# Query projections of a fused attention and expert kernel: two whole-array heads per product, or half-array products of 64 rows

## The chip, the cores and the metric

The kernel runs on one core of a Trainium2 chip. The time is the device time of one execution in microseconds (us), the median of several runs. The core's engines are TensorE (PE in the profile, its weight loads apart as PEld), VectorE (DVE), ScalarE (ACT), GpSimd (POOL) and SyncE (SP, which issues most transfers).

## The reference

Three layers follow each other: attention with a feature map, a gated feed-forward layer, and a layer of slot experts. The change is in the first.

```python
def phi(x):                                   # x: q or k, (4, 8, 576, 64)
    proj = einsum('bhsd,df->bhsf', x, w_phi)  # 64 -> 128 features
    proj = proj - max(abs(proj), axis=-1)
    return concatenate([exp(proj), exp(-proj)], axis=-1)
q_p, k_p = phi(q), phi(k)
kv  = einsum('bhsf,bhsd->bhfd', k_p, v);  z = sum(k_p, axis=2)
num = einsum('bhsf,bhfd->bhsd', q_p, kv)
den = einsum('bhsf,bhf->bhs', q_p, z) + 1e-6
x = num / den                                 # -> 2304 tokens x 512
xn = x / sqrt(mean(x*x) + 1e-6) * rms_g       # gated layer
x = (silu(xn @ w_gate) * (xn @ w_val)) @ w_out
...                                           # slot experts on x
```

## The kernel before, in words

The 2304 tokens are cut into 18 tiles of 128 and into 6 blocks of 384 (three tiles each). The program has three stages.

The **key loop** (lines 502 to 697, to about 123 us of the trace) runs over the 18 tiles. For each it loads the keys and values, projects the keys (`Front.project`, line 519; VectorE then takes the largest value per row, `mx`, and subtracts it into `pr`), takes the exponentials `kp` on ScalarE, and adds to `kacc` (lines 571 and 580). Two things are laid into this loop. One is the conversion of the weights of the gated layer into two float32r parts (class `Conv`: `wt` on ScalarE and VectorE, the casts of line 119 on ScalarE, the low parts of line 122 on GpSimd). The other is the whole attention of query block 0, class `Rows`.

The **gated layer** (lines 738 to 1062) runs over the six blocks. Each block has twelve rounds of a `pg` group (12 products of 384 columns), a `pv` group (12 more) and an `acc` group (9 products of 512 columns). After each group `fill` calls what is planned for that slot, 36 slots per block. Into its first block (123 to 221 us) the attention of query block 1 is laid, class `Turned`; the later query blocks are projected in another way (`Reduced`, `Added`) and are not touched. The **slot experts** come last.

Query blocks 0 and 1 have their features on the columns and their tokens on the partitions. A query tile of heads is `qraw`: two heads' 64 rows one above the other, 384 tokens. There are four of them per block, one per column group c. `project` (line 409) makes one product per token tile i: 128 rows against `wbd_f`, a block diagonal matrix of 128 x 256, so both heads' 128 features come out side by side, and half of what is multiplied is zero. VectorE takes the largest of each head's row (`qmx`, line 415) and subtracts it (`qpr`, line 416). `turn` (line 421) transposes the two heads on TensorE (`T`, line 427) and ScalarE takes the exponentials into `e` (line 429). `attend` makes numerator and denominator: in `Rows` with tokens on the partitions (`o`, line 472, then `y`), in `Turned` with tokens on the columns (`num`, `den`, lines 221 and 249). `scale` and `out` normalize and, in `Rows`, transpose `y` back into `xraw`, the input of the gated layer.

A float32 product is recorded as two instructions (passes) on TensorE, so 24 projections are 48 records. The keys' projection (line 526) is already written with half the array: heads of 64 rows, those of even heads in the upper half and those of odd heads in the lower.

When a step may run is set by two tables, `TURNED0` for block 0 (in half-steps of the key loop) and `TURNED1` for block 1 (in slots). A scheduler then orders each engine's instructions. `P`, `T`, `o`, `yT`, `num` and `den` share an accumulator tag, "misc", with three buffers.

Of the kernel before, what the change touches and what calls it, by code (L numbers as in the profile page):

```python
# [7 lines left out]
F32 = mybir.dt.float32  # L8
F32R = mybir.dt.float32r
U32 = mybir.dt.uint32  # L10
AF = mybir.ActivationFunctionType
ALU = mybir.AluOpType
AX = mybir.AxisListType
# [3 lines left out]
NB, NH, SEQ, HD, DF = 4, 8, 576, 64, 128  # L17
NT, DM, DFF = 2304, 512, 1536
# [3 lines left out]
BLK = 384  # L22
NBLK = NT // BLK
TPB = BLK // 128
# [12 lines left out]
ADDED = [-3, -3, -1, 0, 2, 3, 6, 1, 5, 4, 8, 9, 12, 6, 11, 9, 14, 15, 18, 12, 17, 15, 20, 21, 25, 26, 28, 31]  # L37
TURNED0 = [2, 8, 14, 20, 12, 15, 20, 26, 28, 31]
TURNED1 = [0, 7, 14, 21, 6, 13, 20, 26, 28, 30]

# [25 lines left out]
def tile_kernel(ctx: ExitStack, tc: tile.TileContext, q2T, qT, kT, v, wbd, wg, wv, wo, rmsg, phi, w1, w2, consts, out):  # L66
# [32 lines left out]
    xp = pool(qctx, "xp", side="right")  # L99
# [91 lines left out]
    xraw = {}  # L191
# [209 lines left out]
    class Turned(Q):  # L401
# [6 lines left out]

        def project(self, c, i):
            p = self.psum("P", [128, 2, DF])  # L410
            o = p.rearrange("p h f -> p (h f)")
            PE.matmul(out=o, lhsT=self.raw[c][:, 128 * i:128 * i + 128], rhs=wbd_f, start=True, stop=True)
            mx = self.sp.tile([128, 2, 1], F32, tag="mx", name="qmx", bufs=2)
            self.pr = self.sp.tile([128, 2, DF], F32, tag="pr", name="qpr", bufs=self.bufs["pr"])
            DVE.tensor_reduce(out=mx, in_=p, axis=AX.X, op=ALU.max, apply_absolute_value=True)
            DVE.tensor_tensor(out=self.pr, in0=p, in1=mx.to_broadcast([128, 2, DF]), op=ALU.subtract)
            if i == TPB - 1:
                self.load(c + self.bufs["raw"])
            return self.pr

        def turn(self, c, i, pr):
            if i == 0:
                self.e2 = self.sp.tile([128, 2, 2, BLK], F32, tag="e", name="e2", bufs=self.bufs["e"])
                self.e[2 * c], self.e[2 * c + 1] = self.e2[:, 0], self.e2[:, 1]
            tp = self.psum("T", [128, 2, 128])
            for h in range(2):
                PE.transpose(out=tp[:, h], in_=pr[:, h], identity=ident)
            for s in range(2):
                ACT.activation(out=self.e2[:, :, s, 128 * i:128 * i + 128], in_=tp, func=AF.Exp, scale=1.0 - 2.0 * s)
# [13 lines left out]

        def steps(self, at, attend, end, lag=2):


            r, pr = [], {}

            def p(c, i):
                pr[c, i] = self.project(c, i)  # L450

            for c in range(4):
                for i in range(TPB):
                    r.append((at[c] + i, lambda c=c, i=i: p(c, i)))
                    r.append((at[c] + i + lag, lambda c=c, i=i: self.turn(c, i, pr[c, i])))
                r.append((attend[c], lambda c=c: self.attend(c)))
            r += [(end[0], self.scale), (end[1], self.out)]
            return sorted(r, key=lambda x: x[0])

    class Rows(Turned):  # L460


        def attend(self, c):
            if c == 0:
                self.y = self.sp.tile([128, TPB, 4, 2, HD], F32, tag="y", name="y", bufs=1)
            e = [self.e.pop(2 * c), self.e.pop(2 * c + 1)]
# [9 lines left out]
            DVE.reciprocal(out=rd, in_=rd)  # L476
            DVE.tensor_tensor(out=self.y[:, :, c], in0=o[:, :, :, 0:HD], in1=rd.to_broadcast([128, TPB, 2, HD]), op=ALU.mult)
            for b, t0, t1 in block_parts(self.blk):
# [4 lines left out]
        def scale(self):  # L483
            sq = self.sp.tile([128, 2, 2, BLK], F32, tag="e", name="sq", bufs=self.bufs["e"]).rearrange("p a b t -> p (a b t)")
            ms = self.sp.tile([128, TPB], F32, tag="ms", name="ms", bufs=1)
            rows = [self.y[:, i].rearrange("p c h d -> p (c h d)") for i in range(TPB)]
            for i in range(TPB):
                ACT.activation(out=sq[:, DM * i:DM * i + DM], in_=rows[i], func=AF.Square, accum_out=ms[:, i:i + 1])
            DVE.tensor_scalar(out=ms, in0=ms, scalar1=1.0 / DM, scalar2=1e-6, op0=ALU.mult, op1=ALU.add)
# [4 lines left out]
        def out(self):  # L494
            xraw[self.blk] = xp.tile([128, 4, BLK], F32, tag="xraw", name="xraw", bufs=1)
            for c in range(4):
                tp = self.psum("yT", [128, TPB, 128])
                for i in range(TPB):
                    PE.transpose(out=tp[:, i], in_=self.y[:, i, c].rearrange("p h d -> p (h d)"), identity=ident)
                ACT.activation(out=xraw[self.blk][:, c].rearrange("p (i t) -> p i t", i=TPB), in_=tp, func=AF.Copy, scale=rms_sb[:, c:c + 1])  # L500

    with ExitStack() as pk:
# [146 lines left out]
        q0 = Rows(sp, psk, 0, {"misc": 3, "raw": 2, "pr": 3, "e": 2})  # L649
        qsteps = q0.steps(TURNED0[0:4], TURNED0[4:8], TURNED0[8:])  # L650
        qsteps = [[f for m, f in qsteps if m == n] for n in range(2 * TILES)]
# [86 lines left out]
    with ExitStack() as p2:  # L738
# [233 lines left out]
        steps = []  # L972
        q = Turned(q1p, ps, 1, {"misc": 3, "raw": 2, "pr": 4, "e": 1})
        q.begin()
        qnext = q.steps(TURNED1[0:4], TURNED1[4:8], TURNED1[8:], lag=3)
        for _ in range(2):
# [235 lines left out]
```

## Time and profile before

| | |
|---|---|
| runs | 728.85, 731.23, 732.27 us; median 731.23 |
| the profiled execution | 730.81 us, its span 729.0 us, mean granted TensorE clock 0.991 of full speed |
| TensorE | busy 706.5 us (97%), 4713 products |
| VectorE | busy 447.2 us (61%) |
| ScalarE | busy 340.5 us (47%) |
| projections `P` of query blocks 0 and 1 (line 412) | 48 records, 379 ns each |
| keys' projections `P` (line 526) | 288 records, 272 ns each |
| transposes `T` (line 427) | 48 records, 272 ns each |

The duration of one product includes its way through the array, which overlaps the next product. What a product costs in a stream is read from when the next one starts, or from the chain's pieces. The span is the time from the first to the last instruction of the profiled execution.

### The profile page before, as it was taken

The numbers are of one execution on the slowest core, as the hardware profiler recorded it, in microseconds if no ns is written. First come the engines' busy times: TensorE is split into PE (matmuls) and PEld (weight loads), VectorE is DVE, ScalarE is ACT, GpSimd is POOL, SyncE is SP. The second block draws the span as 40 slices with busy tenths as digits, with TensorE's granted clock in tenths as the row PEclk, the third lists the DMA queues.
The fourth block names the chain that finished last, engine by engine and source line by source line (L and its number), as shares of the span: only waits on it lengthen the run. The fifth ranks groups of instructions, "written<-read, shape, count | busy, mean of one in ns | idle before, by whom it ended". The sixth has DMA issues, their size and how long they took to land.

```text
span 729.0 us, 11925 instructions
## 1 busy us (share of the span) xinstructions
PE 706.5 (97%) x4713; PEld 575.7 (79%) x4713; DVE 447.2 (61%) x874; ACT 340.5 (47%) x711; POOL 170.2 (23%) x84
## 2 busy tenths in 40 slices
PE   6999999999999999999999999999999999999994
PEld 4657766988889888898889888899887999898343
DVE  5899755798655565566776666766667653233313
ACT  5896755698444554355531545415454131212103
POOL 0233200234101210124443244342443300000000
PEclk9999999999999999999999999999999999999898
DMA  8684214443011000100000100001000066576798
GB/s 315 215 293 171 88 37 160 150 181 119 1 62 39 27 22 23 39 22 22 23 1 9 44 22 23 1 9 33 23 1 1 9 259 260 201 261 265 280 371 273
DMA packets 25143, 79.43 MB, mean 109 GB/s; under 512 B 2688, under 2 KB 13376, under 8 KB 18688
## 3 DMA queue, kind: packets, MB, share of 16 engines
q1 hardware_dynamic: 24864, 77.79, 30.0%
q10 hardware_dynamic: 224, 0.88, 0.4%
q8 instruction: 37, 0.61, 0.3%
q14 instruction: 18, 0.15, 0.1%
HBM read 71.99 MB, written 6.67 MB: 108 GB/s over the span
## 4 chain that ended last, share of the span: by engine, by line
PE 84%; DVE 7%; ACT 4%; issue 2%; POOL 1%; DMA 1%; SPq 0%; DVEq 0%; POOLq 0%; ACTq 0%
PE pv L938 20%; PE pg L938 19%; PE acc L963 6%; PE acc L964 6%; PE acc L965 6%; PE num L221 4%; PE kacc L571 4%; PE y L1084 2%; PE P L526 2%; PE kacc L580 2%; PE y L1100 2%; DVE wt L154 2%; DVE wt L156 1%; PE o L472 1%; ACT wt L144 1%
## 5 line engine op out<-in xcount | busy, mean ns | idle before, releaser
L938 PE MATMUL pv<-xnh,wv 128*128 128x384 f32 x576 | 152.3, 345 | 0.0
L938 PE MATMUL pg<-xnh,wg 128*128 128x384 f32 x576 | 150.1, 342 | 0.5 <-DVE t L946 0.3
L938 PEld LDWEIGHTS pv<-xnh,wv 128*128 128x128 f32 x576 | 102.7, 188 | 12.3 <-issue 7.8
L938 PEld LDWEIGHTS pg<-xnh,wg 128*128 128x128 f32 x576 | 104.7, 188 | 6.2 <-ACT xnh L119 0.6
L938 PE MATMUL pv<-xnl,wv 128*128 128x384 f32 x288 | 97.8, 340 | 0.0
L938 PE MATMUL pg<-xnl,wg 128*128 128x384 f32 x288 | 97.5, 339 | 0.0
L963 PE MATMUL acc<-wo,hh 128*128 128x512 f32 x216 | 88.9, 412 | 0.0
L306 POOL PARTITION_ALL_REDUCE qe<-qe x32 | 51.3, 1603 | 155.1 <-ACT qe L305 155.1
L964 PE MATMUL acc<-wo,hh 128*128 128x512 f32 x216 | 85.8, 397 | 0.0
L965 PE MATMUL acc<-wo,hl 128*128 128x512 f32 x216 | 85.5, 396 | 0.0
L946 DVE SCALAR_TENSOR_TENSOR t<-t,pg 128x384 f32<-128x384 f32 x72 | 39.7, 551 | 70.1 <-ACT t L945 70.0
L119 ACT CAST hh<-t 128x384 fp32r<-128x384 f32 x72 | 36.8, 511 | 94.3 <-PE acc L964 73.6
L351 POOL PARTITION_ALL_REDUCE qe<-qe x24 | 61.9, 2626 | 71.3 <-DVE qe L350 41.8
L122 DVE TENSOR_TENSOR hl<-t,hh 128x384 fp32r<-128x384 f32 x72 | 41.8, 581 | 54.7 <-ACT hh L119 45.5
L945 ACT ACTIVATE t<-pg 128x384 f32<-128x384 f32 x72 | 35.2, 489 | 63.8 <-PE pg L938 63.7
L950 DVE TENSOR_TENSOR t<-t,pv 128x384 f32<-128x384 f32 x72 | 39.5, 549 | 30.3 <-PE pv L938 29.7
L938 PEld LDWEIGHTS pg<-xnl,wg 128*128 128x128 f32 x288 | 54.0, 188 | 0.5 <-DVE xnl L122 0.3
L938 PEld LDWEIGHTS pv<-xnl,wv 128*128 128x128 f32 x288 | 54.0, 188 | 0.4 <-issue 0.3
L965 PEld LDWEIGHTS acc<-wo,hl 128*128 128x128 f32 x216 | 40.5, 188 | 9.9 <-DVE hl L122 0.3
L963 PEld LDWEIGHTS acc<-wo,hh 128*128 128x128 f32 x216 | 40.7, 189 | 7.9 <-ACT hh L119 0.9
L964 PEld LDWEIGHTS acc<-wo,hh 128*128 128x128 f32 x216 | 40.7, 189 | 6.4
L571 PE MATMUL kacc<-kp,vt 128*64 128x256 f32 (+1 forms) x320 | 43.2, 393 | 1.9 <-ACT kp L548 1.4
(213 smaller groups left out, 1099.7 us busy)
## 6 DMA issues: line engine op xcount, KB each, us to landing
eu<-in_w_dram SPq DMA_DIRECT2D x32, 1024.0 KB, 6.5
wraw<-in_wg_dram SPq DMA_DIRECT2D x6, 1024.0 KB, 5.0
wraw<-in_wv_dram SPq DMA_DIRECT2D x6, 1024.0 KB, 5.4
wraw<-in_wo_dram SPq DMA_DIRECT2D x6, 1024.0 KB, 4.9
qraw<-in_qT_dram SPq DMA_DIRECT2D x32, 192.0 KB, 2.4
raw<-in_kT_dram SPq DMA_DIRECT2D x18, 256.0 KB, 3.9
vt<-in_v_dram SPq DMA_DIRECT2D x18, 256.0 KB, 3.5
out_dram<-ob SPq DMA_DIRECT2D x18, 256.0 KB, 3.2
```

Of the source, the lines that this page charges most:

```text
L119: ACT.copy(out=hi, in_=src)
L122: (lo_eng or POOL).tensor_tensor(out=lo, in0=src, in1=hi.bitcast(F32), op=ALU.subtract)
L306: POOL.partition_all_reduce(e[:, 0], e[:, 1], channels=128, reduce_op=bass_isa.ReduceOp.absmax)
L351: POOL.partition_all_reduce(e[hh][:, 1], u, channels=128, reduce_op=bass_isa.ReduceOp.add)
L571: PE.matmul(out=kva[o0:o0 + 64, hh // 2], lhsT=self.vt[r0:r1, h], rhs=kp[r0:r1, hh].rearrange("p s f -> p (s f)"), start=first and hh < 2, ...
L938: PE.matmul(out=p, lhsT=w[:, a, c], rhs=x, start=n == 0, stop=n == 11)
L945: ACT.activation(out=t, in_=g, func=AF.Tanh, scale=0.5)
L946: DVE.scalar_tensor_tensor(out=t, in0=t, scalar=1.0, in1=g, op0=ALU.add, op1=ALU.mult)
L950: DVE.tensor_tensor(out=t, in0=t, in1=wide("v", m, xs), op=ALU.mult)
L963: PE.matmul(out=acc[i], lhsT=hh[:, s], rhs=w[:, 0], start=m == 0, stop=False)
L964: PE.matmul(out=acc[i], lhsT=hh[:, s], rhs=w[:, 1], start=False, stop=False)
L965: PE.matmul(out=acc[i], lhsT=hl[:, s], rhs=w[:, 0], start=False, stop=m == MF - 1)
```

## The change

It concerns query blocks 0 and 1 alone. A step now takes two column groups at once, index k, and makes four products of 64 rows for a token tile: the upper heads of the two groups go to one accumulator, the lower heads to another. The largest value and the subtraction are taken per accumulator, so their number and size stay. There are 6 steps per block with two accumulators each, where there were 12 with one. `pr` holds two groups (four heads). `turn` takes its group out of it. The tables now give a place for each of the six projections, for each group's turn, and for attend, scale and out. The projections of groups 0 and 1 come together at the front and those of groups 2 and 3 in the middle; the two later `qraw` loads go out together. In `Rows` the tile `y` is gone: attend writes to `xraw`, scale works in it, and out transposes it in place.

```diff
-TURNED0 = [2, 8, 14, 20, 12, 15, 20, 26, 28, 31]
-TURNED1 = [0, 7, 14, 21, 6, 13, 20, 26, 28, 30]
+TURNED0 = [[2, 3, 4], [14, 15, 16]], [4, 8, 16, 20], [12, 15, 20, 26], [28, 31]
+TURNED1 = [[0, 1, 2], [10, 12, 15]], [3, 8, 17, 22], [6, 13, 20, 26], [28, 30]
...
-        def project(self, c, i):
-            p = self.psum("P", [128, 2, DF])
-            o = p.rearrange("p h f -> p (h f)")
-            PE.matmul(out=o, lhsT=self.raw[c][:, 128 * i:128 * i + 128], rhs=wbd_f, start=True, stop=True)
-            mx = self.sp.tile([128, 2, 1], F32, tag="mx", name="qmx", bufs=2)
-            self.pr = self.sp.tile([128, 2, DF], F32, tag="pr", name="qpr", bufs=self.bufs["pr"])
-            DVE.tensor_reduce(out=mx, in_=p, axis=AX.X, op=ALU.max, apply_absolute_value=True)
-            DVE.tensor_tensor(out=self.pr, in0=p, in1=mx.to_broadcast([128, 2, DF]), op=ALU.subtract)
+        def project(self, k, i):
+            p = [self.psum("P", [128, 2, DF]) for _ in range(2)]
+            for c in range(2):
+                for hf in range(2):
+                    r = slice(64 * hf, 64 * hf + 64)
+                    PE.matmul(out=p[hf][:, c], lhsT=self.raw[2 * k + c][r, 128 * i:128 * i + 128], rhs=wbd_f[r, DF * hf:DF * hf + DF], start=True, stop=True)
+            pr = self.sp.tile([128, 2, 2, DF], F32, tag="pr", name="qpr", bufs=self.bufs["pr"])
+            for hf in range(2):
+                mx = self.sp.tile([128, 2, 1], F32, tag="mx", name="qmx", bufs=2)
+                DVE.tensor_reduce(out=mx, in_=p[hf], axis=AX.X, op=ALU.max, apply_absolute_value=True)
+                DVE.tensor_tensor(out=pr[:, :, hf], in0=p[hf], in1=mx.to_broadcast([128, 2, DF]), op=ALU.subtract)
             if i == TPB - 1:
-                self.load(c + self.bufs["raw"])
-            return self.pr
+                for c in range(2):
+                    self.load(2 * k + c + self.bufs["raw"])
+            return pr
...
-                PE.transpose(out=tp[:, h], in_=pr[:, h], identity=ident)
+                PE.transpose(out=tp[:, h], in_=pr[:, c % 2, h], identity=ident)
...
-        def steps(self, at, attend, end, lag=2):
+        def steps(self, at, turn, attend, end):
...
+            for k in range(2):
+                for i in range(TPB):
+                    r.append((at[k][i], lambda k=k, i=i: p(k, i)))
             for c in range(4):
                 for i in range(TPB):
-                    r.append((at[c] + i, lambda c=c, i=i: p(c, i)))
-                    r.append((at[c] + i + lag, lambda c=c, i=i: self.turn(c, i, pr[c, i])))
+                    r.append((turn[c] + i, lambda c=c, i=i: self.turn(c, i, pr[c // 2, i])))
...
-                self.y = self.sp.tile([128, TPB, 4, 2, HD], F32, tag="y", name="y", bufs=1)
+                xraw[self.blk] = xp.tile([128, 4, BLK], F32, tag="xraw", name="xraw", bufs=1)
...
-            DVE.tensor_tensor(out=self.y[:, :, c], in0=o[:, :, :, 0:HD], in1=rd.to_broadcast([128, TPB, 2, HD]), op=ALU.mult)
+            DVE.tensor_tensor(out=xraw[self.blk][:, c].rearrange("p (i h d) -> p i h d", i=TPB, h=2), in0=o[:, :, :, 0:HD], in1=rd.to_broadcast([128, TPB, 2, HD]), op=ALU.mult)
...
-                    PE.transpose(out=tp[:, i], in_=self.y[:, i, c].rearrange("p h d -> p (h d)"), identity=ident)
+                    PE.transpose(out=tp[:, i], in_=xraw[self.blk][:, c, 128 * i:128 * i + 128], identity=ident)
...
-        q = Turned(q1p, ps, 1, {"misc": 3, "raw": 2, "pr": 4, "e": 1})
+        q = Turned(q1p, ps, 1, {"misc": 3, "raw": 2, "pr": 3, "e": 1})
```

The order of the instructions follows. In its rows a line gives the program's line, the operation, what is written from what, the shape of the result and a count. Lines of the changed program are two to four higher than those of before.

TensorE in the key loop, from the third tile's kacc on, before (`P` from `qraw` is a query projection, `P` from `raw` a key projection):

```order
L580 MATMUL kacc_194<-kp,small 32x256 x7
L412 MATMUL P<-wbd_f,qraw 128x256 x2
L571 MATMUL kacc_192<-kp,vt 64x256 x3
L526 MATMUL P<-wbd_f,raw 128x128 x8
L571 MATMUL kacc_192<-kp,vt 64x256
L571 MATMUL kacc_193<-kp,vt 64x256 x4
L580 MATMUL kacc_194<-kp,small 32x256 x8
L427 MATMUL T<-cst,qpr 128x128 x2
L412 MATMUL P<-wbd_f,qraw 128x256
```

and with the change:

```order
L583 MATMUL kacc_194<-kp,small 32x256 x7
L414 MATMUL P<-wbd_f,qraw 128x128 x6
L574 MATMUL kacc_192<-kp,vt 64x256
L529 MATMUL P<-wbd_f,raw 128x128 x7
L414 MATMUL P<-wbd_f,qraw 128x128 x2
L529 MATMUL P<-wbd_f,raw 128x128
L574 MATMUL kacc_192<-kp,vt 64x256 x3
L574 MATMUL kacc_193<-kp,vt 64x256 x4
L583 MATMUL kacc_194<-kp,small 32x256 x8
L414 MATMUL P<-wbd_f,qraw 128x128 x4
L431 MATMUL T<-cst,qpr 128x128 x2
```

Three steps of four products take the place of three products. The first step and the first half of the second (one row group) stand together; the second half stands among the keys' products.

TensorE in the first round of the gated layer, around the first acc group, before:

```order
L938 MATMUL pv<-xnl_1429,wv_390 128x384
L412 MATMUL P<-wbd_f,qraw 128x256
L963 MATMUL acc_1474<-wo_545,hh 128x512
L964 MATMUL acc_1474<-wo_545,hh 128x512
L965 MATMUL acc_1474<-wo_545,hl 128x512
...
L965 MATMUL acc_1476<-wo_545,hl 128x512
L412 MATMUL P<-wbd_f,qraw 128x256
L938 MATMUL pg<-xnh_1416,wg_692 128x384 x2
```

and with the change:

```order
L941 MATMUL pv<-xnl_1434,wv_413 128x384
L414 MATMUL P<-wbd_f,qraw 128x128 x2
L966 MATMUL acc_1479<-wo_567,hh 128x512
L414 MATMUL P<-wbd_f,qraw 128x128 x2
L967 MATMUL acc_1479<-wo_567,hh 128x512
L968 MATMUL acc_1479<-wo_567,hl 128x512
...
L968 MATMUL acc_1481<-wo_567,hl 128x512
L414 MATMUL P<-wbd_f,qraw 128x128 x4
L941 MATMUL pg<-xnh_1421,wg_695 128x384 x2
```

Each former single product is a group of four half-array products between whole-array ones; here one such group is split in two.

ScalarE ahead of the third attend's numerator in the same block, before (`e` from `T` are the exponentials, `xraw` from `num` is the first reading of the numerator):

```order
L945 ACTIVATE t<-pg 128x384
L429 ACTIVATE e_1947<-T 128x2x128 x2
L119 CAST wo_2234<-wt 128x1024
L429 ACTIVATE e_1947<-T 128x2x128 x2
L119 CAST hh<-t 128x384
L251 COPY xraw<-num 128x384
```

and with the change:

```order
L948 ACTIVATE t<-pg 128x384
L433 ACTIVATE e_1976<-T 128x2x128 x2
L119 CAST wv_2155<-wt 128x1024
L433 ACTIVATE e_1976<-T 128x2x128 x2
L119 CAST wo_2245<-wt 128x1024
L119 CAST hh<-t 128x384
L251 COPY xraw<-num 128x384
```

The last exponentials have moved ahead of the cast of wo; the cast of wv has moved between the last two pairs.

## Rows read from the trace of the kernel before

**Rows 1.** The page, part 1: busy time, share of the span and instructions of each engine.
```profile
PE 706.5 (97%) x4713; PEld 575.7 (79%) x4713; DVE 447.2 (61%) x874; ACT 340.5 (47%) x711; POOL 170.2 (23%) x84
```

**Rows 2.** Stages: us, then busy us of PE, PEld, DVE, ACT, POOL; PEclk; DMA share, GB/s.
```profile
20.00:40.00 20.00, 20.00 (x192) 11.85 (x194) 18.39 (x26) 16.60 (x28) 5.85 (x3) 1.00 0.66 222
40.00:60.00 20.00, 18.72 (x188) 13.04 (x182) 19.56 (x29) 17.91 (x31) 6.52 (x3) 1.00 0.72 258
...
80.00:100.00 20.00, 20.00 (x216) 13.33 (x212) 12.85 (x27) 10.31 (x24) 4.69 (x2) 1.00 0.19 54
...
125.00:150.00 25.00, 25.00 (x156) 22.80 (x155) 19.27 (x26) 17.93 (x29) 7.22 (x3) 1.00 0.52 180
```

**Rows 3.** Timeline, PE, key loop: start, us, engine, line, xcount [idle before <- releaser].
```profile
44.50 0.70 PE L412 MATMUL P<-wbd_f,qraw 128*128 128x256 f32 x2 [1.28 <-DVE kv L617]
...
72.34 1.95 PE L571 MATMUL kacc<-kp,vt 128*64 128x256 f32 x16 [0.49 <-ACT kvs L595]
```

**Rows 4.** Timeline, PE and then ACT, gated layer: num of the third attend.
```profile
185.49 0.87 PE L221 MATMUL num<-e,kv 128*64 128x192 f32 x8 [1.20 <-ACT e L429]
...
185.06 0.65 ACT L429 ACTIVATE e<-T 128x256 f32<-128x256 f32 x2
```

**Rows 5.** Chain in order of time: start, us, engine, line, count of instructions.
```profile
128.21 2.12 PE pg L938 x12
132.45 0.43 PE P L412 x2
...
204.22 2.33 PE pg L938 x12
```

**Rows 6.** Timeline, PE, key loop: half-array groups and what follows each.
```profile
28.00 1.16 PE L526 MATMUL P<-wbd_f,raw 64*128 64x128 f32 x8
29.08 0.65 PE L571 MATMUL kacc<-kp,vt 128*64 128x256 f32 x2
...
36.86 1.16 PE L526 MATMUL P<-wbd_f,raw 64*128 64x128 f32 x16
37.95 1.94 PE L571 MATMUL kacc<-kp,vt 64*64 64x256 f32 x16
```

**Rows 7.** Timeline, PE, 40 to 46 us: a half-array group of four passes.
```profile
45.13 0.49 PE L526 MATMUL P<-wbd_f,raw 64*128 64x128 f32 x4
```

**Rows 8.** Chain, kvt groups; then the lines table, kv copies on VectorE.
```profile
80.62 0.59 PE kvt L608 x4
...
121.35 1.47 PE kvt L608 x12
...
L617 DVE COPY kv<-kvt 128x256 f32<-128x256 f32 x4 | 1.7, 422 | 0.7 <-ACT kv L619 0.7
```

**Rows 9.** Timeline, PE, start of the gated layer; then the chain, one acc product.
```profile
123.47 0.61 PE L938 MATMUL pg<-xnh,wg 128*128 128x384 f32 x2 [0.23 <-ACT xnh L119]
...
133.59 0.23 PE acc L963
```

**Rows 10.** Timeline, ACT, 172 to 188 us: the cast of wo.
```profile
184.11 1.04 ACT L119 CAST wo<-wt 128x1024 fp32r<-128x1024 f32 x1 [2.96 <-DVE wt L156]
```

**Rows 11.** Timeline, DVE, key loop.
```profile
19.89 1.29 DVE L530 TENSOR_REDUCE mx<-P 128x4 f32<-128x512 f32 x2 [0.92 <-PE P L526]
...
22.29 0.75 DVE L415 TENSOR_REDUCE qmx<-P 128x2 f32<-128x256 f32 x2
22.95 0.75 DVE L416 TENSOR_TENSOR qpr<-P,qmx 128x256 f32<-128x256 f32 x2
...
24.63 1.29 DVE L530 TENSOR_REDUCE mx<-P 128x4 f32<-128x512 f32 x2 [0.93 <-PE P L526]
...
29.19 0.69 DVE L530 TENSOR_REDUCE mx<-P 128x4 f32<-128x512 f32 x1 [0.61 <-PE P L526]
```

**Rows 12.** Timeline, PE and ACT, around the first attend of block 1.
```profile
145.92 0.86 PE L249 MATMUL den<-e,kv 128*32 128x192 f32 x16
...
154.02 0.53 ACT L228 ACTIVATE s<-xraw 128x384 f32<-128x384 f32 x1
```

More of the change, by code (lines that the diff above doesn't have):

```diff
@@ L442, in begin, with p @@
                 self.load(c)
-        def steps(self, at, attend, end, lag=2):
+        def steps(self, at, turn, attend, end):
             r, pr = [], {}
-            def p(c, i):
-                pr[c, i] = self.project(c, i)
+            def p(k, i):
+                pr[k, i] = self.project(k, i)
+            for k in range(2):
+                for i in range(TPB):
+                    r.append((at[k][i], lambda k=k, i=i: p(k, i)))
             for c in range(4):
                 for i in range(TPB):
-                    r.append((at[c] + i, lambda c=c, i=i: p(c, i)))
-                    r.append((at[c] + i + lag, lambda c=c, i=i: self.turn(c, i, pr[c, i])))
+                    r.append((turn[c] + i, lambda c=c, i=i: self.turn(c, i, pr[c // 2, i])))
                 r.append((attend[c], lambda c=c: self.attend(c)))
@@ L485, in scale @@
             ms = self.sp.tile([128, TPB], F32, tag="ms", name="ms", bufs=1)
-            rows = [self.y[:, i].rearrange("p c h d -> p (c h d)") for i in range(TPB)]
+            rows = [xraw[self.blk][:, :, 128 * i:128 * i + 128] for i in range(TPB)]
             for i in range(TPB):
-                ACT.activation(out=sq[:, DM * i:DM * i + DM], in_=rows[i], func=AF.Square, accum_out=ms[:, i:i + 1])
+                ACT.activation(out=sq[:, DM * i:DM * i + DM].rearrange("p (c t) -> p c t", c=4), in_=rows[i], func=AF.Square, accum_out=ms[:, i:i + 1])
             DVE.tensor_scalar(out=ms, in0=ms, scalar1=1.0 / DM, scalar2=1e-6, op0=ALU.mult, op1=ALU.add)
@@ L494, in out @@
         def out(self):
-            xraw[self.blk] = xp.tile([128, 4, BLK], F32, tag="xraw", name="xraw", bufs=1)
             for c in range(4):
@@ L649, in tile_kernel @@
         q0 = Rows(sp, psk, 0, {"misc": 3, "raw": 2, "pr": 3, "e": 2})
-        qsteps = q0.steps(TURNED0[0:4], TURNED0[4:8], TURNED0[8:])
+        qsteps = q0.steps(*TURNED0)
         qsteps = [[f for m, f in qsteps if m == n] for n in range(2 * TILES)]
@@ L972, in tile_kernel @@
         steps = []
-        q = Turned(q1p, ps, 1, {"misc": 3, "raw": 2, "pr": 4, "e": 1})
+        q = Turned(q1p, ps, 1, {"misc": 3, "raw": 2, "pr": 3, "e": 1})
         q.begin()
-        qnext = q.steps(TURNED1[0:4], TURNED1[4:8], TURNED1[8:], lag=3)
+        qnext = q.steps(*TURNED1)
         for _ in range(2):
```

## The prediction

> **What bounds the kernel now.** I read the page's busy shares first, then the table of stages, then where TensorE waits. TensorE is busy 97% of the span and VectorE 61% [rows 1]. TensorE's granted clock is 1.00, its upper level (2.4 GHz), in every stretch that I use [rows 2]. So a change counts if it shortens TensorE's own list or the few waits in it. The projections sit in two stages: block 0's in the key loop (to about 123 us), block 1's in the first block of the gated layer (123 to 221 us). The table shows that they differ. From 20 to 60 us VectorE is nearly as full as TensorE (18.39 and 19.56 of 20 us); from 80 us on it has room (12.85 of 20), and early in the gated layer's first block it is busy 19.27 of 25 us [rows 2].
>
> In the key loop a projection waited 1.28 us at 43 us for a VectorE copy to free its accumulator, and kacc waited 0.49 us at 72 us behind a ScalarE copy that stood behind the weight conversion [rows 3]. In block 0 of the gated layer the largest is 1.20 us at 184 us, num waiting for ScalarE's exponentials [rows 4].
>
> **The price of a product.** A whole-array projection of 256 columns is two passes and costs 0.43 us [rows 5]. The half-array form is already in this kernel: the keys use it. Sixteen passes of it (eight products, alternating halves) take 37.95 − 36.86 = 1.09 us; eight passes that were split off in one half alone take 29.08 − 28.00 = 1.08 us [rows 6]. So two halves do run side by side, and unpaired passes cost as much time as pairs. Per pair of passes: (1.16 − 0.49) / 6 = 0.112 us, from the groups of 16 and of 4 [rows 6, 7]. A step with its four products is 8 passes, 4 pairs, 0.45 us, against 0.86 us for the two whole-array products it replaces.
>
> The pairs alone do not make 1.09 us: 8 x 0.112 = 0.90, so **entering** the half-array form costs 0.19 us, called 0.20 below. Returning costs too: twelve pg products behind another pg or pv group take 2.12 us, behind den, whose products fill 32 columns of the array each, 2.33 [rows 5], so 0.21 us. A return to a short whole-array group costs 0.15 (kvt: 4 passes 0.59, 12 passes 1.47, so 0.11 each and 0.15 over [rows 8]). A lone visit between whole-array products is thus 0.45 + 0.20 + 0.21 = 0.86 us: what it replaces.
>
> **Term 1, key loop.** Removed: 12 x 0.43 = 5.16 us. Added: 6 steps x 0.45 = 2.69 us. The order of instructions splits two of the steps (six products, then two) so that both halves' products of one row group follow each other; I add 4 unpaired passes at each of the two places, 8 x 0.112 = 0.90 us. In the order TensorE enters the half-array form 19 times before and 23 after, the whole-array form 19 and 18 times: 4 x 0.20 − 0.15 = +0.65 us. The gain is 5.16 − 2.69 − 0.90 − 0.65 = **0.92 us**, or 1.82 us if every pass finds a partner. Not all reaches the end. The first half's gain comes ahead of the two waits named above [rows 3], which end by VectorE and ScalarE work that is not shortened; time saved ahead of them becomes a longer wait. I keep half, **−0.46 us**.
>
> **Term 2, gated layer, block 0.** Here whole-array work stands on both sides. Removed: 12 x 0.43 = 5.16 us. The order gives the six steps as eight visits (one product, three, two and two, then four times four): 26 pass times, 2.91 us; 8 entries, 1.60; 7 returns at 0.21 and one at 0.15, 1.62. Together 6.13 us, **+0.97 us**. The first visit stands ahead of pg's wait of 0.23 us for xnh [rows 9], which covers about 0.20 of it: **+0.77 us**.
>
> **Term 3, num's wait.** The 1.20 us that end at 185.49 were spent on ScalarE's last pair of exponentials of that group, from 185.06 [rows 4]; in ScalarE's order they stand right behind a cast of wo, which waited 2.96 us for a VectorE join and ran from 184.11 to 185.15 [rows 10]. In the changed order all exponentials of this group stand ahead of that cast; behind it is only hh, needed after num. I take the wait as gone, **−1.20 us**; bounds −1.20 and 0 (the cast of wv, now just ahead, waits as long).
>
> **VectorE.** The count of qmx and qpr stays 24 each, 256 elements each, 0.33 us apart [rows 11], so 0.66 us per pair. The new output goes in two runs of 128; kv, in runs of 64, takes 0.42 us for as many elements [rows 8], so no cost. But block 0's second column group moves from 44 to 52 us into 20 to 31 us: three pairs, 2.0 us, ahead of the wait at 43 us. VectorE's idle time there is 0.92 + 0.93 + 0.61 = 2.46 us [rows 11], which covers it: taken at 0, bound +2.0 us.
>
> **Edits at nothing.** y becomes xraw: the same elements on the same engines; xraw's buffer has no earlier user in block 0, and out already waited for each transpose. The two late loads now go out together; their first use is ten half-steps later in block 0, eight slots later in block 1. On SP's queue they stand ahead of some raw and wraw loads: the wait on the last projection is one that the first of them had before.
>
> **Sum.** −0.46 + 0.77 − 1.20 = −0.89 us on the profiled execution's 730.81 us: **729.9 us**. The median of the runs shown is 731.23, 0.42 above that execution; runs differ by 3.4 us, so 0.5% (3.7 us) is about what can be told from no change.
>
> **Rivals.**
>
> *A, the doubling arrives whole (faster).* If entries hide behind the neighbours' last passes and all passes pair, each stage saves 12 x 0.43 / 2 = 2.58 us, together 5.16, and with term 3 the time is 724.5 us. For it: the pairs do run in half the time [rows 6]. Against: the 0.20 and 0.21 us stand in this trace at every change of form I looked at. The Trainium skill, TensorEngine Tiling (Array Packing), Theoretical Speedup, gives up to 2x for a contraction of at most 64 rows; by that alone the sum would be −5.2 us. The trace agrees inside a group and not across its ends.
>
> *B, accumulators run short (slower).* Each step now takes two of the three "misc" accumulators at once, and TensorE, in order, waits at its next product if VectorE or ScalarE is late. In the key loop the 2.0 us moved forward would show in full. In the gated layer the second column's turn follows attend after two slots, where it had four. ScalarE's exponentials cannot start before s is done; for the first attend that was 7.8 us after den ended (146.8 to 154.6) [rows 12]. TensorE gets to the next projection after three groups of 2.12 us [rows 5], one acc group of 9 x 0.23 us [rows 9] and two transposes of two 0.11 us passes, 8.9 us after den; with 0.65 us for a pair of exponentials [rows 4] in between the margin is 0.4 us. One conversion cast (1.04 us [rows 10]) on ScalarE ahead of them turns it into a wait, at up to two places, with about 2.0 us in all. Then 730.81 + 0.97 + 2.0 + 2.0 = 735.8 us. It decides if ScalarE's exponentials start later than 8.2 us after den and VectorE has under 2 us of slack before 43 us. The Trainium skill, TensorEngine Tiling (Array Packing), Gotcha 1: PSUM Pressure, says that row tiling raises the pressure on the accumulators, since row tiles write to different banks; the trace of before, whose query projections take one accumulator each, does not show that price.
>
> *C, the halves do not overlap.* Then every step costs 8 pass times, 0.90 us; 12 steps are 10.8 us against the 6.5 us that I count with unpaired passes, +4.3, 734.2 us. Against it [rows 6]: sixteen passes in the time of eight.
>
> **Chances.** Forecast 0.75, A 0.12, B 0.10, C 0.03. The lower end: all passes paired and none lost (−1.82), the two waits of the key loop gone (−1.77), num's gone (−1.20), term 2 at +0.77: 726.8. The upper: nothing kept from term 1, +0.97, num's wait kept, 2.0 us of VectorE: 733.8. I widen the lower end to 726.4 for part of A. Faster by over 0.5% (under 727.6): A and the low edge of the forecast, 0.15. Slower (over 734.9): B, 0.10. Same 0.75.
>
> **What would show it.** The half-array groups of the projections should take 0.112 us a pair and about 0.4 us more per visit in the gated layer; the key loop should end 0.3 to 1.8 us earlier and the gated layer's first block last 0.8 us longer, less num's wait. Wrong would be: num still waiting over 1 us; a new TensorE idle of over 0.5 us ahead of a projection or transpose named by VectorE or ScalarE (B); or pg behind a projection at 2.12 us (A).

## The result: slower by 0.6%, and the profile after

The change takes 735.52 us against 730.37 us for before (medians of six runs each). The ratio on record is 1.0059 with a 95% interval of 1.0030 to 1.0087; the quotient of the two medians is 1.0071. The forecast was 729.9 us, the range ended at 733.8: both are missed, and the time is 0.3 us from that of rival B. The profiled execution, 732.32 us with a span of 730.5 us, is one of the change's faster ones. (A stretch at the half clock in the last stage differs between profiles, 670 to 690 us at 0.91 here and 0.83 in that of before; so profiles are compared stage by stage, and times by medians.)

TensorE's sums on the page look as before [rows 1]; ScalarE and VectorE have not moved either:

```profile
PE 707.7 (97%) x4761; PEld 575.7 (79%) x4761; DVE 448.0 (61%) x874; ACT 340.6 (47%) x711; POOL 169.8 (23%) x84
```

The difference is seen by stage (columns as in [rows 2]). The key loop is counted from the same place in both kernels, the kacc group right ahead of the first query projection. In before, then in the change, it starts at:

```profile
20.37 1.06 PE L580 MATMUL kacc<-kp,small 128*32 128x256 f32 x14
...
18.76 1.06 PE L583 MATMUL kacc<-kp,small 128*32 128x256 f32 x14
```

First before, from there to the first product of the gated layer, then that layer's first block:

```profile
20.37:123.47 103.10, 100.44 (x1021) 66.27 (x1020) 81.17 (x144) 74.14 (x139) 21.82 (x9) 1.00 0.44 151
...
123.47:219.47 96.00, 93.74 (x569) 82.45 (x570) 71.64 (x115) 63.97 (x122) 23.03 (x9) 1.00 0.31 110
```

and the same two of the change:

```profile
18.76:125.79 107.03, 103.45 (x1046) 68.71 (x1045) 81.68 (x144) 75.56 (x140) 21.36 (x9) 0.95 0.44 151
...
125.79:222.88 97.09, 95.28 (x594) 81.59 (x594) 71.84 (x115) 63.35 (x122) 23.22 (x9) 1.00 0.32 109
```

The key loop takes 3.9 us longer, and the gated layer's first block 1.1 us. (On the trace's own clock the loop ends only 2.3 us later, because this execution reached the first query projection 1.6 us earlier. That start differs between executions: in the second profile of the change, run e4 below, it is 20.21 us, and the loop from there takes 107.74 us, 4.6 more than before's.) The later blocks keep the distance. In the key loop TensorE is idle 3.58 us where it was 2.66, and its granted clock is no longer 1.00 but 0.95. Two short stretches make that, here the windows with TensorE's granted clock in the third column from the end:

```profile
44.00:48.00 4.00, 4.00 (x28) 2.21 (x26) 3.69 (x8) 4.00 (x7) 1.79 (x1) 0.57 0.74 257
...
64.00:72.00 8.00, 8.00 (x46) 6.52 (x48) 4.52 (x10) 3.74 (x5) 2.36 (x1) 0.57 0.13 35
```

TensorE is busy all through them, at the lower level (1.2 GHz) for most of it. The timeline of TensorE shows what stands ahead of each: a wait. (A record is one pass, and a float32 product is two, so x16 is eight products.)

```profile
43.40 0.44 PE L431 MATMUL T<-cst,qpr 128*128 128x128 f32 x2 [1.63 <-ACT e L433]
...
44.63 3.58 PE L574 MATMUL kacc<-kp,vt 128*64 128x256 f32 x16
...
60.72 1.04 PE L414 MATMUL P<-wbd_f,qraw 64*128 64x128 f32 x11
...
63.26 0.68 PE L414 MATMUL P<-wbd_f,qraw 64*128 64x128 f32 x4 [0.94 <-DVE qpr L419]
63.87 4.33 PE L476 MATMUL o<-kv,e 128*128 128x65 f32 x24
68.12 1.23 PE L529 MATMUL P<-wbd_f,raw 64*128 64x128 f32 x8
69.28 3.21 PE L574 MATMUL kacc<-kp,vt 128*64 128x256 f32 x16
```

The sixteen kacc passes that take 1.95 us at the full clock [rows 3] take 3.58 and 3.21 us. Of the two places the second is the dearer. Before's groups kacc at 58.77 and 72.34 us [the latter in rows 3] are those at 57.84 and 76.27 us of the change: 0.9 us ahead in front of the second place, 3.9 us behind after it. Of these 4.9 us the half clock accounts for about 3.2 (from start to start, the o group takes 4.25 us where one at the full clock takes 2.82, the eight keys' passes 1.16 and not 0.65, kacc 3.14 and not 1.88), and 0.94 is the wait. At the first place kacc alone loses 1.6 us. It is no trait of one profile: the mean granted clock was 0.982 to 0.989 in all twelve executions of the change (six here, six of e4), and 0.991 to 0.997 in the 23 of before beside e4.

Both waits are for an accumulator. At 43.40 it holds a transpose, which ScalarE's exponentials free; in ScalarE's order they stand behind a piece of the weight conversion, which waited 1.10 us for its transfer until 40.34. At 63.26 it is VectorE that is late. Its timeline there:

```profile
58.29 1.28 DVE L533 TENSOR_REDUCE mx<-P 128x4 f32<-128x512 f32 x2
59.49 1.28 DVE L537 TENSOR_TENSOR pr<-P,mx 128x512 f32<-128x512 f32 x2
60.68 1.44 DVE L154 SCALAR_TENSOR_TENSOR wt<-wt,wraw 128x1024 uint32<-128x1024 uint32 x1
62.04 0.74 DVE L418 TENSOR_REDUCE qmx<-P 128x2 f32<-128x256 f32 x2
62.70 0.74 DVE L419 TENSOR_TENSOR qpr<-P,qmx 128x256 f32<-128x256 f32 x2
```

The second step's products have begun at once with the first's (11 records from 60.72 us); their accumulators are read only after the keys' mx and pr and a piece of the weight conversion. The next product stands in TensorE's order ahead of the whole o group, and waits until the first qpr has freed a buffer.

### The profile page after: what moved, and what is told of

The parts are those of the page before. It is cut to its first block, busy times and chain, and to the rows that moved or that the text cites. A ratio compares the mean times of both kernels' runs of the same rounds, so it can differ in the third digit from the quotient of the medians.

```text
span 730.5 us, 12029 instructions
## 1 busy us (share of the span) xinstructions
PE 707.7 (97%) x4761; PEld 575.7 (79%) x4761; DVE 448.0 (61%) x874; ACT 340.6 (47%) x711; POOL 169.8 (23%) x84
## 4 chain that ended last, share of the span: by engine, by line
PE 79%; DVE 7%; ACT 6%; DMA 5%; issue 1%; SPq 1%; ACTq 0%; DVEq 0%
PE pv L941 19%; PE pg L941 18%; PE acc L966 6%; PE acc L967 6%; PE acc L968 6%; PE num L221 4%; PE kacc L574 3%; DMA wraw<-in_wv_dram 2%; PE y L1087 2%; PE y L1103 2%; DVE wt L154 1%; DMA wraw<-in_wg_dram 1%; PE kacc L583 1%; PE o L476 1%; DMA wraw<-in_wo_dram 1%
## 5 line engine op out<-in xcount | busy, mean ns | idle before, releaser
L574 PE MATMUL kacc<-kp,vt 128*64 128x256 f32 (+1 forms) x320 | 45.1, 408 | 1.8 <-ACT kp L551 1.8
```

The lines of the kernel that those rows point to most:

```text
L574: PE.matmul(out=kva[o0:o0 + 64, hh // 2], lhsT=self.vt[r0:r1, h], rhs=kp[r0:r1, hh].rearrange("p s f -> p (s f)"), start=first and hh < 2, ...
```

## The experiments

All runs of one batch share the runs of before on their chip: 729.63 us for the first four, 729.64 for the next four, 730.29 for the four after, 729.37 for the last three.

**Which block.** The change again, and with one block put back each time:

```diff
 e1, and project, turn and steps of before for block 0
-TURNED0 = [[2, 3, 4], [14, 15, 16]], [4, 8, 16, 20], [12, 15, 20, 26], [28, 31]
+TURNED0 = [2, 8, 14, 20, 12, 15, 20, 26, 28, 31]
 e2, and project, turn and steps of before for block 1
-TURNED1 = [[0, 1, 2], [10, 12, 15]], [3, 8, 17, 22], [6, 13, 20, 26], [28, 30]
+TURNED1 = [0, 7, 14, 21, 6, 13, 20, 26, 28, 30]
 e4: nothing
```

> Query block 0 (key loop) has its old projections, places and transposes again, with attend still writing to xraw; block 1 (gated layer) is as changed. Theory K (the loss arises in the key loop: steps that take two accumulators make TensorE wait at 41 and 62 us, and the granted clock falls to half behind these waits): about 731.5 us, 1 us over before, no half clock between 13 and 120 us. Rival G (the loss arises in the gated layer's first block, at the eight visits to the half-array form): 733 us or more, as slow as the change. If writing to xraw cost anything, the key loop would end later than 122.9 us.

> The other half: block 0 as changed, block 1 with its old whole-array projections and places. Theory K: 734 to 735 us, with a half-clock stretch between 40 and 75 us and the waits of over 1 us at about 41 and 62 us. Rival G: 730 to 731 us.

> The changed kernel once more, for a second profile and for the spread. Theory K: 735 us, a half-clock stretch between 40 and 75 us again, of 3 to 10 us in all, behind the same two waits. Rival L (the half clock of the first profile was chance): none in that stretch, and a time near 732 us.

Measured: e1 729.81 us (ratio 1.0004, 0.9990 to 1.0018), e2 731.22 (1.0026, 1.0010 to 1.0043), e4 734.71 (1.0069, 1.0045 to 1.0092). The loss needs block 0. But the parts do not add up (0.2 + 1.6 against 5.1 us), although e2's trace has both waits of the key loop (1.43 us at 43.69, 1.67 us at 62.88), and its key loop, counted as above, takes 107.76 us, 4.7 more than before's. What differs is the last stage, which the change does not touch. From the last product of the gated layer to the end, before, then e2:

```profile
671.50:729.02 57.52, 46.07 (x484) 22.82 (x484) 16.59 (x45) 9.29 (x24) 1.80 (x1) 0.88 0.85 304
...
675.47:729.41 53.94, 43.02 (x485) 21.72 (x484) 16.60 (x45) 9.29 (x24) 1.80 (x1) 0.96 0.90 325
```

In these profiles e2 gets 3.6 us back there at a higher granted clock (e4 takes 55.30 us); why that clock differs stays unexplained.

**Form or order.** The changed order with whole-array products, in both blocks (e3) or in block 1 alone, block 0 as before (e9):

```diff
-                for hf in range(2):
-                    r = slice(64 * hf, 64 * hf + 64)
-                    PE.matmul(out=p[hf][:, c], lhsT=self.raw[2 * k + c][r, ...], rhs=wbd_f[r, ...], ...)
+                PE.matmul(out=p[c].rearrange("p h f -> p (h f)"), lhsT=self.raw[2 * k + c][:, ...], rhs=wbd_f, ...)
```

> The changed places and the paired steps with two accumulators, but whole-array products of 256 columns (one accumulator per column group, 12 products per block as before). Theory K: the key loop waits and falls to half clock as with the change, the gated layer's first block is about 1 us shorter than with the change: 733.5 to 735 us. Rival H (the half-array products themselves, with half of the rows at rest, bring the clock down): no half clock in the key loop, 730 to 731.5 us.

> Block 0 old; block 1 with the changed places and paired steps, but whole-array products. Against the run with block 0 old this leaves out only the visits to the half-array form in the gated layer. By the price of a visit (0.86 us against 0.86 us, and three more visits than steps) it is 0.5 to 1.0 us faster than that run: 729 us. If accumulators held by steps cost more there (a whole-array step has each accumulator written later), it is slower than that run, 731 us or more.

Measured: e3 736.58 us (1.0080, 1.0052 to 1.0108), e9 735.59 (1.0083, 1.0060 to 1.0106). Without the half-array form the same order is no faster. This does not clear the form in block 0, though: e9 loses as much as e3 with block 0 as before, so e3's loss may be block 1's. (e6, e10 and e16 below clear it: they keep the form and lose nothing.) e3's profiled execution, at 730.48 us its fastest by over 5 us, shows something else: the waits of the key loop without the half clock. Its key loop, counted as above, and the second wait:

```profile
18.95:123.38 104.43, 100.72 (x1022) 66.63 (x1021) 81.12 (x144) 75.11 (x140) 21.40 (x9) 1.00 0.46 156
```

```profile
64.06 0.67 PE L412 MATMUL P<-wbd_f,qraw 128*128 128x256 f32 x2 [1.29 <-DVE qpr L417]
```

With waits of 1.44 (at 44.88 us) and 1.29 us and the clock at 1.00 it takes 1.3 us more than before's, where the change takes 3.9 and e4 4.6.

e9, which has no half-array product in block 1, was to be faster than e1 and is 5.8 us slower. Its TensorE timeline in the gated layer, then ScalarE's, then VectorE's:

```profile
157.76 0.59 PE L412 MATMUL P<-wbd_f,qraw 128*128 128x256 f32 x2
162.01 1.22 PE L412 MATMUL P<-wbd_f,qraw 128*128 128x256 f32 x2 [3.66 <-ACT e L431]
```

```profile
159.95 1.05 ACT L119 CAST wv<-wt 128x1024 fp32r<-128x1024 f32 x1 [0.68 <-DVE wt L156]
...
161.32 1.18 ACT L431 ACTIVATE e<-T 128x256 f32<-128x256 f32 x4
```

```profile
156.64 3.27 DVE L156 SCALAR_TENSOR_TENSOR wt<-wraw,wt 128x1024 uint32<-128x1024 uint32 x1
```

A step's second product waits 3.66 us for an accumulator that holds a transpose; its exponentials stand behind a cast that waits for VectorE's conversion. From 162 to 168 us the granted clock is 0.55, mostly the lower level. This is rival B's chain in the gated layer, in full. In the change the same place costs 0.15 and 0.22 us. (e3's profile has it too, 2.78 us at 160.26.)

**Fewer or shared accumulators.** Before, with two "misc" buffers in the key loop where it had three (e5); the change with the five accumulators of the keys' projections and of "misc" in one set (e12); before with the same five (e14):

```diff
-        kb = {"tag": "k", "raw": 4, "pr": 3, "P": ("P", 2)}
+        kb = {"tag": "k", "raw": 4, "pr": 3, "P": ("misc", 5)}
...
-        q0 = Rows(sp, psk, 0, {"misc": 3, "raw": 2, "pr": 3, "e": 2})
+        q0 = Rows(sp, psk, 0, {"misc": 5, "raw": 2, "pr": 3, "e": 2})
```

These are the lines of e12 and e14; kvt and the keys' first tile go with them. e5 is before with these (and the keys' first tile at two):

```diff
-        q0 = Rows(sp, psk, 0, {"misc": 3, "raw": 2, "pr": 3, "e": 2})
+        q0 = Rows(sp, psk, 0, {"misc": 2, "raw": 2, "pr": 3, "e": 2})
-                tp = psk.tile([128, 2, 2, 128], F32, tag="misc", name="kvt", bufs=3)
+                tp = psk.tile([128, 2, 2, 128], F32, tag="misc", name="kvt", bufs=2)
```

> The kernel before, with nothing changed but the shared accumulators in the key loop: two in place of three. It has no half-array query products and the old places. Theory W (TensorE's waits for accumulators in the key loop are what costs, first as waits, then as half clock behind them): waits of over 1 us between 20 and 110 us beyond those of before, a half-clock stretch there in most executions (mean clock under 0.990), and 2 to 8 us more than before. Rival F (the clock falls for the form of the products, not for waits): a granted clock of 0.991 as before, and a time longer by the waits alone, under 2 us.

> The change as it is, its places too, but the key loop's five accumulators (two of the keys' projections, three of all else) are one set that all share; a step of two then takes two of five. Theory (accumulators run short): the waits of 1.63 us at 43 us and 0.94 us at 63 us fall by half or more, no half granted clock behind them, and the time falls by 2 us or more, to 730 to 733 us; it can be eaten up in part if the keys' projections now wait instead, which the next run, before with the same five, shows by itself. Rival (VectorE, whose work moved forward by 2.0 us, is late whatever the number of accumulators): the waits stay, named by VectorE, and the time stays at 734.5 to 735.5 us.

> Before, with the same five shared accumulators: what sharing does by itself. Theory: before takes one accumulator per projection and has few waits to lose (1.28 and 0.49 us), so 727.5 to 730.5 us, within 2 us of before. If sharing costs the keys' projections, 732 us or more, and the run before this one is to be read against this instead of against before.

Measured: e5 739.41 us (1.0132, 1.0109 to 1.0155), e12 733.11 (1.0042, 1.0025 to 1.0059), e14 729.27 (0.9983, 0.9963 to 1.0002). An accumulator less, with VectorE's work where it was, costs more than the whole change. TensorE's timeline of e5 has the same kind of waits, here for kv copies and exponentials:

```profile
43.58 0.66 PE L608 MATMUL kvt<-cst,kvs 128*128 128x128 f32 x4 [1.50 <-DVE kv L617]
...
73.64 0.44 PE L427 MATMUL T<-cst,qpr 128*128 128x128 f32 x2 [2.02 <-ACT e L429]
```

Its key loop kept the granted clock at 1.00 and still took 6.2 us longer than before's:

```profile
19.11:128.46 109.35, 104.51 (x1022) 67.46 (x1021) 82.90 (x144) 75.22 (x140) 22.30 (x9) 1.00 0.43 145
```

So a shortage costs without the clock too: 4.84 us idle where before had 2.66. The rest, 4.1 us, is busy time. The order is another one here, with the keys' projections in more and smaller groups; how much of the 4.1 us that explains was not measured. (This profile is e5's fastest execution, with a mean granted clock of 0.991; the other five have 0.984 to 0.987.) e12 lies 2.8 us above its before where e4 lay 5.1 above its own; of the 2.3 us, sharing gave before 1.0 as well, so two more buffers to draw on gave back little of the loss: their number does not decide by itself, VectorE's and ScalarE's delay does with it. There are other waits in the places of the old ones, and PEclk from 64 to 72 us is 0.60: the expectation that the waits would fall by half was wrong.

```profile
37.21 1.94 PE L574 MATMUL kacc<-kp,vt 64*64 64x256 f32 x16 [1.57 <-ACT kvs L598]
...
62.90 4.71 PE L476 MATMUL o<-kv,e 128*128 128x65 f32 x24 [2.53 <-DVE pr L537]
```

**The places.** The change's steps, moved apart. e6 and e7 have block 1 as before, the others the changed one:

```diff
 change: TURNED0 = [[2, 3, 4], [14, 15, 16]], [4, 8, 16, 20], [12, 15, 20, 26], [28, 31]
 e6:     TURNED0 = [[2, 4, 6], [14, 16, 18]], [5, 9, 17, 21], [12, 15, 20, 26], [28, 31]
 e7:     TURNED0 = [[2, 4, 6], [17, 19, 21]], [5, 9, 19, 23], [12, 15, 22, 26], [28, 31]
 e10:    TURNED0 as in e6
 e15:    TURNED0 = [[2, 4, 6], [14, 15, 16]], [5, 9, 16, 20], [12, 15, 20, 26], [28, 31]
 e16:    TURNED0 = [[2, 3, 4], [14, 16, 18]], [4, 8, 17, 21], [12, 15, 20, 26], [28, 31]
```

> Block 0 as changed but with its six projections spread over every second half-step (2, 4, 6 and 14, 16, 18; turns from 5, 9, 17, 21); block 1 old. Every step's four products then stand together. Theory W: the wait at 62 us goes, the key loop stays at full clock or nearly, all pairs are found, and the time is 728 to 729.5 us, 0 to 1.5 us under before. Rival F (the half-array form costs its clock wherever it stands): 731 us or more, as with block 0 changed alone.

> As the run with spread places, but the second three projections still later (17, 19, 21; turns from 19 and 23, third attend at 22), where VectorE has room. Theory W: no wait of over 1 us for an accumulator behind 45 us, full clock, 728 to 729.5 us. If the late group is too late for scale and out at the loop's end, the end of the key loop waits instead, and the time is 730 us or more.

> The change in both blocks; only block 0's six projections stand one half-step apart from each other (2, 4, 6 and 14, 16, 18 in place of 2, 3, 4 and 14, 15, 16; turns one later), so that a step's two accumulators come free before the next step asks for two. Theory (the waits for the three shared accumulators in the key loop, with the half granted clock behind them, are what the change cost): block 0's part comes out at or below before, as it did with block 1 old (729.3), and block 1's changed part adds 0.2 (what it cost with block 0 old) to 1.1 us: 729.5 to 730.5 us, no half granted clock between 40 and 75 us, and no wait of over 1.2 us ahead of a projection or transpose there. Rival (block 1's changed order is what costs, and only showed when the whole was changed): 733 us or more. Rival (the half-array form costs wherever it stands): 734 us.

> The change with only block 0's first three projections spread (2, 4, 6, their turns one half-step later, 5 and 9); the later three stay at 14, 15, 16. If the cost stands mostly at the second place (the wait of 0.94 us at 63 us and the 6.8 us at the half clock behind it; against before, the profile of the change loses 4.9 us from 58 to 72 us and at the first place only 0.8 us from 16 to 45 us), little is gained: 733 to 735 us, the wait at the second place still there. If the first place's wait (1.63 us, then 3.4 us at the half clock) is what makes the second place late, all is gained: 729 to 730 us.

> The change with only the later three spread (14, 16, 18, their turns one half-step later, 17 and 21); the first three stay at 2, 3, 4. If the second place carries most: 729.5 to 731 us, the wait of 1.6 us at 43 us still there, no half granted clock from 58 to 75 us. If the first place does: 733 to 735 us, with the second place's waits where they were.

Measured: e6 729.30 us (0.9991, 0.9971 to 1.0011), e7 729.93 (1.0001, 0.9986 to 1.0016), **e10 728.92** (0.9979, 0.9962 to 0.9997), e15 734.09 (1.0054, 1.0034 to 1.0073), **e16 729.40** (1.0000, 0.9982 to 1.0018). One half-step between block 0's steps takes the whole loss away, and it is the later three that matter: spreading the first three alone gains next to nothing, spreading the later three alone brings the time back to that of before; both together gain 1.4 us more, though the two intervals overlap. TensorE's timeline of e16 at the second place, and the stage behind it:

```profile
59.05 0.71 PE L414 MATMUL P<-wbd_f,qraw 64*128 64x128 f32 x8
59.69 2.89 PE L476 MATMUL o<-kv,e 128*128 128x65 f32 x24
62.52 1.16 PE L529 MATMUL P<-wbd_f,raw 64*128 64x128 f32 x16
63.61 1.95 PE L574 MATMUL kacc<-kp,vt 128*64 128x256 f32 x16
```

```profile
64.00:72.00 8.00, 7.63 (x82) 4.81 (x81) 8.00 (x16) 6.00 (x12) 2.37 (x1) 1.00 0.35 99
```

VectorE does there just what it did in the change:

```profile
57.63 1.28 DVE L533 TENSOR_REDUCE mx<-P 128x4 f32<-128x512 f32 x2
58.82 1.28 DVE L537 TENSOR_TENSOR pr<-P,mx 128x512 f32<-128x512 f32 x2
60.02 1.43 DVE L154 SCALAR_TENSOR_TENSOR wt<-wt,wraw 128x1024 uint32<-128x1024 uint32 x1
61.37 0.74 DVE L418 TENSOR_REDUCE qmx<-P 128x2 f32<-128x256 f32 x2
62.04 0.74 DVE L419 TENSOR_TENSOR qpr<-P,qmx 128x256 f32<-128x256 f32 x2
```

It is the same chain, 0.7 us earlier and no faster. The difference is what TensorE asks for meanwhile: one step instead of two, then an o group that needs one buffer, which is free. The wait at the first place stayed (1.37 us at 43.37), this time with no half clock behind it. In e15 the two steps still stand together, and the wait is longer, since TensorE arrives earlier:

```profile
57.95 1.16 PE L414 MATMUL P<-wbd_f,qraw 64*128 64x128 f32 x12
...
62.46 0.89 PE L414 MATMUL P<-wbd_f,qraw 64*128 64x128 f32 x4 [1.64 <-DVE qpr L419]
63.28 5.38 PE L476 MATMUL o<-kv,e 128*128 128x65 f32 x24
```

```profile
64.00:72.00 8.00, 8.00 (x42) 6.71 (x43) 3.52 (x10) 2.83 (x4) 2.35 (x1) 0.50 0.12 33
```

What the first place saved (kacc 3.7 us ahead of before's at 58.77, 1.4 of it from before the first query projection) became wait and half clock at the second (4.7 us behind at 72.34).

**Two attempts at more.** e11 is e10 with block 1's later steps moved too; e13 is e10 with the five shared accumulators:

```diff
 e11: TURNED1 = [[0, 1, 2], [11, 14, 16]], [3, 8, 17, 22], [6, 13, 20, 26], [28, 30]
 e13: "P": ("misc", 5), and "misc" 5 for kvt and Rows, with e10's TURNED0
```

> As the run before, and block 1's later three projections one slot apart as well (11, 14, 16 in place of 10, 12, 15). If the waits for accumulators are also what keeps block 1 from gaining (0.98 us ahead of the second half of a projection at 157 us when block 0 was old), that wait falls under 0.3 us and the time comes out 0.5 to 1 us below the run before: 728.5 to 730 us. If block 1's cost is the price of the visits (0.8 us by the sum), nothing changes: within 0.4 us of the run before.

> Block 0's six projections spread, block 1 as changed, and the key loop's five accumulators shared. Alone, spreading gave 728.9 and sharing in before 729.3, each some 1 us below before. If what both remove are different waits, they add: 727.5 to 728.5 us. If both remove the same wait (the one at 43 us): 728.9 us within 0.7. If sharing makes other waits, as it did in the change (2.8 us ahead of an o group at 60 us): 730 us or more.

Measured: e11 731.03 us (1.0016, 1.0002 to 1.0030), e13 728.57 (0.9985, 0.9967 to 1.0003). e11 missed: the wait at 157 us went, but a cast of hh came late (TensorE waits 1.29 us at 176.17), and the second half of num waits 1.39 us again, at 188.69; its profile also has a half-clock stretch in the key loop, whose order is e10's. e13 stands with e10, as if both removed the same waits. e10 is the fastest against its own before, by 0.2%, which is less than one can well tell from nothing; against the change, by the two ratios, it is 0.8% faster.

## Why the prediction was wrong, step by step

**The step that failed is the paragraph on VectorE, "taken at 0"**: the sum held no wait for an accumulator in the key loop, which was to gain 0.46 us and lost 3.9. The paragraph looked at the work that moves into 20 to 31 us. That is not what decides: the wait at 43.40 is named by ScalarE, and spreading the first three steps is worth 1.4 us at most (e16 against e10, each by its before). What was not looked at is the second place, 60 us, where VectorE is full [rows 2] and two steps, which want four accumulators of three, stand in a row in TensorE's order. The prediction weighed VectorE's amount of work and not the number of buffers that TensorE holds while VectorE is busy with other things. e16 shows that it is this: same VectorE work, one step less asked for, no wait there.

**The clock behind the waits had no term.** Each stretch was taken at the full clock because before's rows were [rows 2]. In the change's key loop the groups at the lower level cost 4.8 us (1.6 at the first place, 3.2 at the second) and the idle time rose by 0.9; what remains to the measured 3.9 is a gain of 1.8 from the shorter products.

**Term 1's own size was right.** A step of eight passes takes 0.64 us with its entry (e16: 59.05 to 59.69), 0.65 by the sum. In e10, where no step is split and no wait reaches a microsecond, the two stages read:

```profile
19.27:119.88 100.61, 98.52 (x1045) 65.45 (x1044) 78.95 (x144) 74.39 (x140) 23.12 (x9) 1.00 0.46 159
...
119.88:216.93 97.05, 95.30 (x594) 81.62 (x595) 71.83 (x115) 63.33 (x123) 23.23 (x9) 1.00 0.31 109
```

The key loop is 2.5 us shorter than before's: TensorE's busy time fell by 1.92 us, for which Term 1 had 1.82 if every pass finds a partner, and its idle time by 0.57. (This is e10's fastest execution; but e6, with the same block 0, has a busy time of 98.49 us.) The change takes 6.4 us longer there than e10: 1.5 us of it idle, and the other 4.9 nearly all the half clock.

**Term 2 was right.** The chain of the change shows the visits:

```profile
132.47 0.64 PE P L414 x6
133.11 2.31 PE pv L941 x12
135.42 0.64 PE P L414 x4
136.06 0.42 PE acc L966
```

0.64 us into the form and 0.19 us back (pv 2.31 against 2.12, acc 0.42 against 0.23 [rows 5, 9]): 0.83 us a visit for 0.86 predicted. In the gated layer's first block TensorE's busy time rose by 95.28 − 93.74 = 1.54 us, some 0.6 us over the +0.97; where those 0.6 lie was not traced.

**Term 3 was half right.** Num's wait is gone; its sixteen passes run through:

```profile
188.59 1.61 PE L221 MATMUL num<-e,kv 128*64 128x192 f32 x16
```

But the block's idle time fell only from 2.26 to 1.81 us, by 0.45 and not 1.20: the rest came back in small waits of a projection, a transpose and pg (0.15, 0.22 and 0.56 us, the last for VectorE's t at 198.53 us). So this block gave +1.1 us where −0.43 was forecast. The sum's miss of 5.6 us is mostly the key loop's (4.4 us by these profiles), 1.5 us are this.

**Rival B was the case, at another place and another price.** It foresaw 2.0 us in the key loop and 2.0 us in the gated layer, and got 735.8 us; that this lies 0.3 us from the measured time is luck. The mechanism is shown (e10, e15, e16, with e5 for the shortage by itself), and VectorE's lack of slack decided, at 60 us and not before 43. The prediction's own sign for it, an idle time of over 0.5 us ahead of a projection or transpose named by VectorE or ScalarE, came twice (1.63 and 0.94 us). The gated layer's wait that it describes is near nothing in the change, and 3.66 us in e9. The key loop's price was higher since the granted clock halved behind the waits. A chance of 0.10 was too low: the accumulators that a stretch of TensorE's order asks for can be counted in that order, and two steps of two stood in a row against three buffers. That the halves might not overlap (rival C), or that the gain would arrive whole (rival A), no run bears out.

The Trainium skill, TensorEngine Tiling (Array Packing), Gotcha 1: PSUM Pressure, says that row tiles write to different banks and cannot access the same one at once, and that this raises the pressure. The runs agree on the pressure, though here it came from taking two accumulators per step in either form (e9 waits with whole-array products too): the loss is about 5 us with three buffers and steps close together, and nothing measurable with steps apart. The Trainium skill, TensorE: Matmul & The Clock Gate, A second HAM failure mode: psum-queue depth-cycling, tells of a kernel whose clock moved between its levels because TensorE idled briefly and often while cycling through accumulators. The rows at 43 and 63 us agree in kind, but a single wait stands ahead of each, and other waits as long had no lower clock behind them (e3, e10, e16).

**Open** stays why the clock falls behind some of these waits and not behind others, so that the price of a wait cannot be forecast from these runs, why the last stage's clock differs between kernels, and what whole-array products at the changed places would cost in block 0 alone, which no run has with block 1 as before.

## What to carry to other kernels

Before packing two heads into one step, count in the in-order engine's list how many accumulators it asks for between two points at which the reading engine is busy with something long; if the count passes the buffers, the gain turns into a wait there. Moving the steps apart by one slot is then worth more than the packing (6 us here, while the packing with its steps apart gains 1.4 us at most on before). A sum that prices only the waits can be too low: here the lower clock behind them cost more than they did. A shortened stretch ahead of such a wait gives nothing: what e15 gained at the first place it lost at the second.

## What was not expected of the hardware

Waits of 0.94 to 1.64 us on TensorE were followed by several microseconds at 1.2 GHz: 0.57 of full speed from 64 to 72 us in the change, 0.50 in e15. Not every such wait is. e16 waits 1.37 us at 43.37 and e3 1.44 and 1.29 us in the key loop, both at the full clock. And e10 and e11 have the same instructions in the key loop and the same wait of 0.94 us ahead of a keys' projection (67.79 us in e10, 68.81 in e11). e10 kept the full clock, e11 did not; here e11, TensorE and then the stage behind:

```profile
68.81 1.13 PE L529 MATMUL P<-wbd_f,raw 64*128 64x128 f32 x10 [0.94 <-DVE pr L537]
69.87 3.53 PE L574 MATMUL kacc<-kp,vt 128*64 128x256 f32 x16
```

```profile
70.00:74.00 4.00, 4.00 (x28) 1.94 (x31) 3.51 (x5) 3.41 (x8) 0.00 (x0) 0.57 0.20 66
```

What decides it, no run here settles; e11 had one more wait, 0.64 us at 46.73.
